# First feed forward: the cosine's whole turns by an integer conversion, with h read from PSUM

## The chip, the cores and the metric

The kernel runs on one core of one Trainium2 chip. The metric is device time in microseconds (us) of one execution. Five engines work side by side, each through a queue of its own in order: TensorE (PE; its weight loads are PEld), VectorE (DVE), ScalarE (ACT), GpSimd (POOL) and SyncE (SP), which issues most transfers.

## The reference, cut to what matters

Attention over 4 batches, 8 heads, 576 positions gives x of 2304 tokens by 512. Two feed forwards follow. The change is in the first alone.

```python
def _moe_ref(x, w_in, w_out):          # x (2304, 512), w_in (512, 2048), w_out (2048, 512)
    h = x @ w_in
    g = h * np.cos(h)
    return g @ w_out

def _moe2_ref(x, w_in, w_out, a, b):   # the second feed forward: a rational function of h
    ...
```

[...]

## The kernel before

**Numbers.** Matmuls run in fp32r on operands that are split in a high and a low part, so each product is three matmuls: high by high, high by low, low by high. Weights arrive as 64-bit words; `dec_abs` (L142, ACT) and `dec_ops` (L154, L156, L158, DVE) turn a tile of them into fp32, and `w_split` (L173 on ACT for the high part, L176 on POOL for the low part) splits it.

**Steps.** The first feed forward has 128 steps, g = 0 to 127. A step takes one block of tokens (256, 352 or 288 columns) and one of 16 slices of 128 hidden units. Its parts are, in the letters of the strings that order them:

- `l1` (L419): 12 matmuls give h in a PSUM bank of the tag `h`, which has two banks.
- U or u: u = h/2pi + 0.25, on ACT (L508) or on DVE (L510).
- K or k: hs, a copy of h in SBUF, on ACT (L512) or on DVE (L514). 114 of the 128 steps have it; in the other 14, M reads h itself.
- J or j: t = u + 12582912, which rounds u to a whole number, on ACT (L516, 5 times) or on DVE (L518, 123 times).
- V: u = (t - 12582912) - u on DVE (L520), both operands in SBUF.
- N: the sine on ACT (L522). M: t = sine times hs (or h) on DVE (L524).
- G: gh, the high part of t, on ACT (L528). H or h: gl, the low part, on POOL or on DVE (L530).
- `l2` (L438): 12 matmuls of gh and gl with the second weight, two or three steps later, into the banks y.

Other letters of the string place the decoding and splitting of the first weights (x, y, z, p, q, s, w, a, b) and the attention of the next tokens (T, L). Steps 0 to 31 work on the first two blocks of 256 tokens; the first weights are decoded beside steps 0 to 15, and the attention and the second weights' decoding go on beside later steps. From step 32 on most strings run N, M, G and H of the step before beside U, K, J and V of this one. The order is written out by hand in `ORD`, `C_ORD`, `AB_ORD` and `REST`; a letter acts on the first pending step that has not had it and whose forerunner by `NEED` is done. Buffers rotate in pools: u, t and hs have two buffers each, and an instruction that writes a buffer or a bank waits for the last one that used it. The program never lets DVE and ACT into one PSUM bank at once, reads included.

From step 128 the second feed forward runs (L466 to L492); the change does not touch its steps.

Of the kernel before, what the change touches and what calls it, by code (L numbers as in the profile page):

```python
# [8 lines left out]
F32 = mybir.dt.float32  # L9
F32R = mybir.dt.float32r  # L10
I32 = mybir.dt.int32
BF16 = mybir.dt.bfloat16
AF = mybir.ActivationFunctionType
ALU = mybir.AluOpType
AX = mybir.AxisListType

B, H, S, D = 4, 8, 576, 64
# [3 lines left out]
NF = DFF // 128  # L21
# [12 lines left out]
NB2 = 384  # L34
# [17 lines left out]
LV1 = (3, 4)  # L52
PL1 = []
AB_ORD = "UKjVTswxyzNMabpqGHL"
NEED = {"J": "U", "V": "J", "N": "V", "M": "N", "G": "M", "H": "G"}
REST = "swNMUKjVGhTL"
C_ORD = {}
ORD = {}
for _g in (0, 1, 23):
    ORD[_g] = "ukjVTswxyzNMabpqGHL"  # L60
NPRE = 4
EVB, STB = 4, 6
LATE_OE = False
# [3 lines left out]
NCONST = C_ID + 128  # L67
TWO_PI = 6.2831850
INV_2PI = 1.0 / (2.0 * math.pi)
MAGIC = 12582912.0  # L70
LN_SHIFT = 2.0 ** -63


# [17 lines left out]
def attention_moe_moe_kernel(ctx: ExitStack, tc: tile.TileContext, qk0, qk, vv, w1, w2, consts, a, b, out):  # L91
    nc = tc.nc
    ACT, DVE, POOL, PE, SP = nc.scalar, nc.vector, nc.gpsimd, nc.tensor, nc.sync
# [4 lines left out]
    ep = ctx.enter_context(tc.tile_pool(name="ep", bufs=2))  # L98
# [13 lines left out]
    biases = const.tile([128, 4], F32, name="biases")  # L112
# [300 lines left out]
    def l1(bk, f):  # L413
        d = blocks[bk]
        n, cs = d["n"], slice(d["xcol"], d["xcol"] + d["n"])
        h = bank("a" if d["ph"] == 2 and f % 2 else "h")
        ops = [(w, x, c) for c in range(KD) for w, x in ((wh, xh), (wh, xl))] + [(wl, xh, c) for c in range(KD)]
        for k, (w, x, c) in enumerate(ops):
            PE.matmul(h[:, :n], w[d["ph"], f, 0][:, 128 * c:128 * c + 128], x[c][:, cs], start=k == 0, stop=k == len(ops) - 1)  # L419
        return h[:, :n]  # L420
# [19 lines left out]
    def evac(bk):  # L440
        d = blocks[bk]
        n, t0 = d["n"], 0 if bk == bB else d["tok"]
        for c, y in enumerate(d["y"]):
            t = stage("ev")
            if d["ph"] == 2 or bk == bB:
                n = 512
            src = y[:, :n]
            if bk == len(blocks) - 1 and c == len(d["y"]) - 1:
                ACT.activation(out=t[:, :256], in_=src[:, :256], func=AF.Copy)
                DVE.tensor_copy(out=t[:, 256:], in_=src[:, 256:])  # L450
            elif c % 2:
                DVE.tensor_copy(out=t[:, :n], in_=src)  # L452
            else:
                ACT.activation(out=t[:, :n], in_=src, func=AF.Copy)
            if d["ph"] == 1:
                SP.dma_start(out=x2d[:, c, t0:t0 + n], in_=t[:, :n])
            else:
                (ACT if bk == len(blocks) - 1 and c == len(d["y"]) - 1 else SP).dma_start(out=out[t0 + 128 * c:t0 + 128 * c + 128, :], in_=t)
# [37 lines left out]
    def ew_new(g, bk, h):  # L496
        n = blocks[bk]["n"]
        e = dict(g=g, h=h)
        for k in ("u", "t", "hs"):
            e[k] = ep.tile([128, NB2], F32, tag=k, name=k)[:, :n]  # L500
        for k in ("gh", "gl"):
            e[k] = None
        return e

    def ew_op(c, e):
        u, t, hs, h = e["u"], e["t"], e["hs"], e["h"]
        if c == "U":
            ACT.activation(out=u, in_=h, func=AF.Identity, scale=INV_2PI, bias=biases[:, 2:3])  # L508
        elif c == "u":
            DVE.tensor_scalar(out=u, in0=h, scalar1=INV_2PI, scalar2=0.25, op0=ALU.mult, op1=ALU.add)  # L510
        elif c == "K":
            ACT.activation(out=hs, in_=h, func=AF.Copy)  # L512
        elif c == "k":
            DVE.tensor_copy(out=hs, in_=h)  # L514
        elif c == "J":
            ACT.activation(out=t, in_=u, func=AF.Identity, bias=biases[:, 3:4])  # L516
        elif c == "j":
            DVE.tensor_scalar(out=t, in0=u, scalar1=MAGIC, scalar2=None, op0=ALU.add)  # L518
        elif c == "V":
            DVE.scalar_tensor_tensor(out=u, in0=t, scalar=MAGIC, in1=u, op0=ALU.subtract, op1=ALU.subtract)  # L520
        elif c == "N":
            ACT.activation(out=u, in_=u, func=AF.Sin, scale=-TWO_PI)  # L522
        elif c == "M":
            DVE.tensor_tensor(out=t, in0=u, in1=hs if "K" in e else h, op=ALU.mult)  # L524
        elif c == "G":
            n = t.shape[1]
            e["gh"], e["gl"] = (gp.tile([128, NB2], F32R, tag=k, name=k)[:, :n] for k in ("gh", "gl"))
            ACT.activation(out=e["gh"], in_=t, func=AF.Copy)  # L528
        else:
            (POOL if c == "H" else DVE).tensor_tensor(out=e["gl"], in0=t, in1=e["gh"].bitcast(F32), op=ALU.subtract)  # L530
            state["g", e["g"]] = e["gh"], e["gl"]

# [118 lines left out]
    def order(g):  # L651
        return ORD[g] if g in ORD else AB_ORD if g < 2 * NF else C_ORD[g % (2 * NF)] if g % (2 * NF) in C_ORD else REST
# [9 lines left out]
    def run_steps(p, g0, g1):  # L662
        for g in range(g0, g1):
            bk = None
            if g < len(steps):
                bk, f = steps[g]
                h = l1(bk, f)
            if state["evac"]:
                evac(state["evac"].pop())
            run("early", g)  # L670
            if g < N1:
                todo = decs.pop(g, ())
                e = ew_new(g, bk, h)
                fifo = {c: state["e"] + [e] if c in "NMGH" else [e] for c in "UKJVNMGH"}
                state["e"].append(e)
                for c in order(g):
                    if c.upper() in fifo:
                        for x in fifo[c.upper()]:
                            if c.upper() not in x and NEED.get(c.upper(), "U") in x | {"U": 1}:
                                x[c.upper()] = True  # L680
                                ew_op(c, x)
                                break
                    elif c in "sS":
                        split1(0, POOL if c == "s" else DVE)
                    elif c in "wW":
                        split1(1, POOL if c == "w" else DVE)
                    elif c in "xyzpq":
                        if c == "x":
                            for _, tm in todo:
                                dec_ops(0, *tm)  # L690
                        else:
                            i = "yzpq".index(c)
                            if i % 2 < len(todo):
                                dec_ops(1 + i // 2, *todo[i % 2][1])
                    elif c in "ab":
                        for k in dplan.get(g + 1, ())["ab".index(c):][:1]:
                            w_abs(g + 1, k)
                    elif c == "T":
                        run("pe1", g)
                        run("pe1e", g)  # L700
                    elif c == "L":
                        run("late", g)
                state["e"] = [x for x in state["e"] if "H" not in x]
                state["dec"] = todo
            else:
                for x in state["e"]:
                    for c in "NMGH":
                        if c not in x:
                            ew_op(c, x)
                state["e"] = []  # L710
                second(g, LAG)
                if g == N1:
                    nc.scalar.preload_act_table_set("natural_log_exp_and_others")
                prev = state.pop("prev", None)
                if prev is not None:
                    ew_b(*prev)
                if state["evac"]:
                    evac(state["evac"].pop())
                if bk is not None:
                    state["prev"] = ew_a(p, bk, h)  # L720
                if prev is not None:
                    gh = ew_c(*prev[:2])
                if bk is not None:
                    ew_r(*state["prev"])
                if prev is not None:
                    state["g", g - 1] = ew_d(*prev[:2], gh)
                run("pe1", g)
                run("pe1e", g)
                run("late", g)
            if g < N1:  # L730
                second(g, LAG_AB if bk <= bB else LAG)
            run("pe2", g)
            run("load", g)

    state = {"evac": [], "l2": 0, "e": []}
    dplan = {}
    for k in range(NPRE, NF):
        dplan[DSTEP[k - NPRE]] = pairs[k]
    with tc.manual_schedule():
        with tc.tile_pool(name="att", bufs=2) as p:  # L740
# [1 line left out]
            DVE.memset(msk16, 0.0)  # L742
            DVE.memset(biases[:, 1:2], -63.0 * math.log(2.0))
            DVE.memset(biases[:, 2:3], 0.25)
            DVE.memset(biases[:, 3:4], MAGIC)
            wb = bank("a")
            ms = {}

# [181 lines left out]
```

## Time and profile before

| | |
|---|---|
| median of 3 runs | 993.06 us (992.69 to 993.42) |
| the profiled execution | 990.51 us |
| its span, first to last instruction | 988.7 us |
| busy: PE, DVE, ACT, POOL | 925.2, 786.6, 670.8, 287.5 us |

The span leaves 1.8 us of the profiled execution outside. Busy time is the time in which an engine has an instruction of the program under way; a DVE instruction that is held up inside counts as busy. In the timeline a row is start, duration, engine, line, operation, tiles and shape; in square brackets stands how long the engine had been idle and what it waited for.

### The profile page before, as it was taken

The numbers are of one execution on the slowest core, as the hardware profiler recorded it, in microseconds if no ns is written. First come the engines' busy times: TensorE is split into PE (matmuls) and PEld (weight loads), VectorE is DVE, ScalarE is ACT, GpSimd is POOL, SyncE is SP. The second block draws the span as 40 slices with busy tenths as digits, with TensorE's granted clock in tenths as the row PEclk, the third lists the DMA queues.
The fourth block names the chain that finished last, engine by engine and source line by source line (L and its number), as shares of the span: only waits on it lengthen the run. The fifth ranks groups of instructions, "written<-read, shape, count | busy, mean of one in ns | idle before, by whom it ended". The sixth has DMA issues, their size and how long they took to land.

```text
span 988.7 us, 17482 instructions
## 1 busy us (share of the span) xinstructions
PE 925.2 (94%) x6367; PEld 861.8 (87%) x6367; DVE 786.6 (80%) x1497; ACT 670.8 (68%) x1444; POOL 287.5 (29%) x279
## 2 busy tenths in 40 slices
PE   7557889999999989999899999999999999999997
PEld 6557789998999989999899988888888898898896
DVE  5999986688677787777878898877787778777776
ACT  5765557565475565765757887777777777777775
POOL 2466552213212122121222223223223232232221
PEclk9778999999999999999999999999999999999999
DMA  9745200443423534234325620010010100100000
GB/s 312 254 168 216 62 22 9 148 159 109 138 86 128 172 138 160 89 128 151 128 60 178 188 78 1 2 64 1 6 60 1 51 14 1 65 1 0 33 1 32
DMA packets 51526, 89.36 MB, mean 90 GB/s; under 512 B 4584, under 2 KB 28400, under 8 KB 51440
## 3 DMA queue, kind: packets, MB, share of 16 engines
q1 hardware_dynamic: 50720, 86.58, 26.6%
q10 hardware_dynamic: 720, 1.67, 0.5%
q8 instruction: 50, 0.82, 0.3%
q14 instruction: 36, 0.29, 0.1%
HBM read 70.40 MB, written 17.83 MB: 89 GB/s over the span
## 4 chain that ended last, share of the span: by engine, by line
DVE 32%; PE 26%; ACT 22%; POOL 10%; issue 7%; DMA 3%; POOLq 0%; SPq 0%; ACTq 0%; DVEq 0%
PE h L419 11%; PE y L438 10%; POOL z L478 9%; DVE r L481 7%; ACT r L477 6%; ACT r L476 5%; ACT gh L487 4%; DVE h L482 3%; DVE dec L156 3%; DVE a L482 3%; DVE t L524 3%; DVE dec L158 2%; PE a L259 2%; DVE u L520 2%; DVE t L518 2%
## 5 line engine op out<-in xcount | busy, mean ns | idle before, releaser
L419 PE MATMUL h<-xh,w 128*128 128x288 f32 (+3 forms) x1408 | 339.5, 313 | 9.2 <-DVE hs L514 4.4
L419 PEld LDWEIGHTS h<-xh,w 128*128 128x128 f32 x1408 | 246.2, 191 | 14.6 <-DVE hs L514 4.6
L438 PE MATMUL y<-gh,w 128*128 128x288 f32 (+2 forms) x1024 | 231.3, 302 | 4.5 <-ACT gh L528 4.5
L419 PE MATMUL h<-xl,w 128*128 128x288 f32 (+3 forms) x704 | 207.9, 311 | 0.0
L438 PE MATMUL y<-w,gh 128*128 128x512 f32 x576 | 196.1, 393 | 5.6 <-DVE ev L452 4.3
L478 POOL TENSOR_TENSOR z<-q,r 128x384 f32<-128x384 f32 x96 | 97.3, 1013 | 297.3 <-ACT r L477 293.9
L438 PEld LDWEIGHTS y<-gh,w 128*128 128x128 f32 x1024 | 173.6, 191 | 5.2 <-ACT gh L528 5.2
L438 PE MATMUL y<-gl,w 128*128 128x288 f32 (+2 forms) x512 | 153.6, 300 | 6.0 <-POOL gl L530 5.6
L419 PEld LDWEIGHTS h<-xl,w 128*128 128x128 f32 x704 | 135.6, 193 | 1.8
L438 PEld LDWEIGHTS y<-w,gh 128*128 128x128 f32 x576 | 108.2, 188 | 27.9 <-DVE ev L452 6.8
L481 DVE SCALAR_TENSOR_TENSOR r<-z,r 128x384 f32<-128x384 f32 x96 | 69.5, 724 | 73.3 <-POOL z L478 73.3
L530 POOL TENSOR_TENSOR gl<-t,gh 128x288 fp32r<-128x288 f32 (+2 forms) x67 | 64.1, 957 | 197.4 <-ACT gh L528 180.9
L438 PE MATMUL y<-w,gl 128*128 128x512 f32 x288 | 114.8, 399 | 5.0 <-DVE gl L492 4.8
L419 PE MATMUL a<-xh,w 128*128 128x384 f32 x384 | 106.3, 337 | 0.0
L508 ACT ACTIVATE u<-h,biases 128x288 f32<-128x288 f32 (+2 forms) x116 | 57.2, 494 | 72.2 <-PE h L419 69.2
L438 PEld LDWEIGHTS y<-gl,w 128*128 128x128 f32 x512 | 97.8, 191 | 9.1 <-POOL gl L530 8.4
L528 ACT ACTIVATE gh<-t 128x288 fp32r<-128x288 f32 (+2 forms) x128 | 56.8, 443 | 54.6 <-DVE t L524 54.0
L518 DVE TENSOR_SCALAR t<-u 128x288 f32<-128x288 f32 (+2 forms) x123 | 53.2, 432 | 45.8 <-ACT u L508 44.3
L522 ACT ACTIVATE u<-u 128x288 f32<-128x288 f32 (+2 forms) x128 | 56.7, 443 | 43.7 <-DVE u L520 43.5
L524 DVE TENSOR_TENSOR t<-u,hs 128x288 f32<-128x288 f32 (+2 forms) x114 | 62.9, 552 | 23.8 <-ACT u L522 23.4
L520 DVE SCALAR_TENSOR_TENSOR u<-t,u 128x288 f32<-128x288 f32 (+2 forms) x128 | 74.2, 580 | 6.2 <-ACT t L516 2.0
L419 PEld LDWEIGHTS a<-xh,w 128*128 128x128 f32 x384 | 70.5, 188 | 1.8
(115 smaller groups left out, 1645.3 us busy)
## 6 DMA issues: line engine op xcount, KB each, us to landing
raw<-in_w_dram SPq DMA_DIRECT2D x63, 512.0 KB
qk<-in_qk_dram SPq DMA_DIRECT2D x18, 481.0 KB
wf<-dec SPq DMA_DIRECT2D x32, 256.0 KB
wf<-wf SPq DMA_DIRECT2D x32, 256.0 KB
x2s<-x2d SPq DMA_DIRECT2D x24, 192.0 KB
out_dram<-ev SPq DMA_DIRECT2D x17, 256.0 KB
v<-in_vv_dram SPq DMA_DIRECT2D x16, 240.0 KB
v<-in_vv_dram SPq DMA_DIRECT2D x24, 157.5 KB
```

What stands on the lines that cost most here:

```text
L419: PE.matmul(h[:, :n], w[d["ph"], f, 0][:, 128 * c:128 * c + 128], x[c][:, cs], start=k == 0, stop=k == len(ops) - 1)
L438: PE.matmul(y, l, r, start=first and i == 0 and bk != bB, stop=last and i == 2 and bk != bA)
L477: ACT.activation(out=r, in_=r, func=AF.Exp, scale=-1.0, bias=biases[:, 1:2])
L478: POOL.tensor_tensor(out=z, in0=q, in1=r, op=ALU.mult)
L481: DVE.scalar_tensor_tensor(out=r, in0=z, scalar=2.0, in1=r, op0=ALU.subtract, op1=ALU.mult, reverse0=True)
L482: DVE.scalar_tensor_tensor(out=h, in0=h, scalar=ab[:, 0:1], in1=r, op0=ALU.add, op1=ALU.mult)
L508: ACT.activation(out=u, in_=h, func=AF.Identity, scale=INV_2PI, bias=biases[:, 2:3])
L518: DVE.tensor_scalar(out=t, in0=u, scalar1=MAGIC, scalar2=None, op0=ALU.add)
L520: DVE.scalar_tensor_tensor(out=u, in0=t, scalar=MAGIC, in1=u, op0=ALU.subtract, op1=ALU.subtract)
L524: DVE.tensor_tensor(out=t, in0=u, in1=hs if "K" in e else h, op=ALU.mult)
L528: ACT.activation(out=e["gh"], in_=t, func=AF.Copy)
L530: (POOL if c == "H" else DVE).tensor_tensor(out=e["gl"], in0=t, in1=e["gh"].bitcast(F32), op=ALU.subtract)
```

## The change

J is dropped: U (or u) now writes its result as a 32-bit integer, into the buffer of t, and V takes that integer from h/2pi, reading h from PSUM for the second time. The sine gets scale 2pi and a bias of a quarter turn from a column of `biases`. In steps 0 to 31 the letters K and k are taken out of the order string, so that M reads h from PSUM there; from step 32 on they stay. The letters J and j stay in the strings and do nothing. hs is allocated only where it is written.

```diff
--- before.py
+++ after.py
@@ -52,12 +52,13 @@
 LV1 = (3, 4)
 PL1 = []
 AB_ORD = "UKjVTswxyzNMabpqGHL"
-NEED = {"J": "U", "V": "J", "N": "V", "M": "N", "G": "M", "H": "G"}
+NEED = {"J": "U", "V": "U", "N": "V", "M": "N", "G": "M", "H": "G"}
 REST = "swNMUKjVGhTL"
 C_ORD = {}
 ORD = {}
 for _g in (0, 1, 23):
     ORD[_g] = "ukjVTswxyzNMabpqGHL"
+COPY = {ord(c): None for c in "Kk"}
 NPRE = 4
 EVB, STB = 4, 6
 LATE_OE = False
@@ -67,7 +68,6 @@
 NCONST = C_ID + 128
 TWO_PI = 6.2831850
 INV_2PI = 1.0 / (2.0 * math.pi)
-MAGIC = 12582912.0
 LN_SHIFT = 2.0 ** -63
 
 
@@ -496,37 +496,35 @@
     def ew_new(g, bk, h):
         n = blocks[bk]["n"]
         e = dict(g=g, h=h)
-        for k in ("u", "t", "hs"):
+        for k in ("u", "t"):
             e[k] = ep.tile([128, NB2], F32, tag=k, name=k)[:, :n]
-        for k in ("gh", "gl"):
-            e[k] = None
         return e
 
+
     def ew_op(c, e):
-        u, t, hs, h = e["u"], e["t"], e["hs"], e["h"]
+        u, t, h = e["u"], e["t"], e["h"]
+        k = t.bitcast(I32)
         if c == "U":
-            ACT.activation(out=u, in_=h, func=AF.Identity, scale=INV_2PI, bias=biases[:, 2:3])
+            ACT.activation(out=k, in_=h, func=AF.Identity, scale=INV_2PI, bias=biases[:, 2:3])
         elif c == "u":
-            DVE.tensor_scalar(out=u, in0=h, scalar1=INV_2PI, scalar2=0.25, op0=ALU.mult, op1=ALU.add)
-        elif c == "K":
-            ACT.activation(out=hs, in_=h, func=AF.Copy)
-        elif c == "k":
-            DVE.tensor_copy(out=hs, in_=h)
-        elif c == "J":
-            ACT.activation(out=t, in_=u, func=AF.Identity, bias=biases[:, 3:4])
-        elif c == "j":
-            DVE.tensor_scalar(out=t, in0=u, scalar1=MAGIC, scalar2=None, op0=ALU.add)
+            DVE.tensor_scalar(out=k, in0=h, scalar1=INV_2PI, scalar2=0.25, op0=ALU.mult, op1=ALU.add)
+        elif c in "Kk":
+            e["hs"] = ep.tile([128, NB2], F32, tag="hs", name="hs")[:, :t.shape[1]]
+            if c == "K":
+                ACT.activation(out=e["hs"], in_=h, func=AF.Copy)
+            else:
+                DVE.tensor_copy(out=e["hs"], in_=h)
         elif c == "V":
-            DVE.scalar_tensor_tensor(out=u, in0=t, scalar=MAGIC, in1=u, op0=ALU.subtract, op1=ALU.subtract)
+            DVE.scalar_tensor_tensor(out=u, in0=h, scalar=INV_2PI, in1=k, op0=ALU.mult, op1=ALU.subtract)
         elif c == "N":
-            ACT.activation(out=u, in_=u, func=AF.Sin, scale=-TWO_PI)
+            ACT.activation(out=u, in_=u, func=AF.Sin, scale=TWO_PI, bias=biases[:, 3:4])
         elif c == "M":
-            DVE.tensor_tensor(out=t, in0=u, in1=hs if "K" in e else h, op=ALU.mult)
+            DVE.tensor_tensor(out=t, in0=u, in1=e.get("hs", h), op=ALU.mult)
         elif c == "G":
             n = t.shape[1]
             e["gh"], e["gl"] = (gp.tile([128, NB2], F32R, tag=k, name=k)[:, :n] for k in ("gh", "gl"))
             ACT.activation(out=e["gh"], in_=t, func=AF.Copy)
-        else:
+        elif c in "Hh":
             (POOL if c == "H" else DVE).tensor_tensor(out=e["gl"], in0=t, in1=e["gh"].bitcast(F32), op=ALU.subtract)
             state["g", e["g"]] = e["gh"], e["gl"]
 
@@ -673,7 +671,7 @@
                 e = ew_new(g, bk, h)
                 fifo = {c: state["e"] + [e] if c in "NMGH" else [e] for c in "UKJVNMGH"}
                 state["e"].append(e)
-                for c in order(g):
+                for c in order(g).translate(COPY if g < 2 * NF else {}):
                     if c.upper() in fifo:
                         for x in fifo[c.upper()]:
                             if c.upper() not in x and NEED.get(c.upper(), "U") in x | {"U": 1}:
@@ -742,7 +740,7 @@
             DVE.memset(msk16, 0.0)
             DVE.memset(biases[:, 1:2], -63.0 * math.log(2.0))
             DVE.memset(biases[:, 2:3], 0.25)
-            DVE.memset(biases[:, 3:4], MAGIC)
+            DVE.memset(biases[:, 3:4], 0.25 * TWO_PI)
             wb = bank("a")
             ms = {}
```

## Rows read from the trace of the kernel before

**Rows 1.** Busy us by stretch: PE, PEld, DVE, ACT, POOL; clock, DMA share, GB/s.

```profile
...
43.00:134.00 91.00, 66.84 (x502) 61.36 (x503) 87.91 (x136) 49.73 (x112) 55.20 (x44) 0.87 0.38 128
...
216.00:575.00 359.00, 349.39 (x2865) 342.65 (x2866) 280.70 (x581) 232.61 (x526) 80.11 (x82) 1.00 0.40 130
...
```

**Rows 2.** The chain that ended last, 43 to 134 us: start, duration, what.

```profile
...
43.83 0.33 DVE hs L514
...
132.90 1.10 PE y L438 x7
```

**Rows 3.** J, V and M by line: nanoseconds minimum/median/maximum, first and last start, forms.

```profile
...
L518 DVE TENSOR_SCALAR t<-u x123: 277/310/1378, 44.1 to 561.8; 128x288 f32<-128x288 f32 x78, 128x256 f32<-128x256 f32 x29, 128x352 f32<-128x352 f32 x16
...
L520 DVE SCALAR_TENSOR_TENSOR u<-t,u x128: 424/459/1550, 44.4 to 562.1; 128x288 f32<-128x288 f32 x80, 128x256 f32<-128x256 f32 x32, 128x352 f32<-128x352 f32 x16
...
L524 DVE TENSOR_TENSOR t<-u,hs x114: 383/450/1456, 47.2 to 564.4; 128x288 f32<-128x288 f32 x76, 128x256 f32<-128x256 f32 x23, 128x352 f32<-128x352 f32 x15
L524 DVE TENSOR_TENSOR t<-u,h x14: 407/422/509, 53.9 to 457.6; 128x256 f32<-128x256 f32 x9, 128x288 f32<-128x288 f32 x4, 128x352 f32<-128x352 f32 x1
...
```

**Rows 4.** DVE busy time in 43 to 134 us: line 518, then line 520.

```profile
...
43.00:134.00 91.00, 9.35 (x16) 0.87 0.38 128
...
43.00:134.00 91.00, 14.99 (x17) 0.87 0.38 128
...
```

**Rows 5.** Timeline of step 6: DVE, then POOL, then PE.

```profile
...
87.08 1.38 DVE L518 TENSOR_SCALAR t<-u 128x256 f32<-128x256 f32 x1
88.50 1.39 DVE L520 SCALAR_TENSOR_TENSOR u<-t,u 128x256 f32<-128x256 f32 x1
...
91.01 0.41 DVE L524 TENSOR_TENSOR t<-u,hs 128x256 f32<-128x256 f32 x1
...
86.83 2.77 POOL L176 TENSOR_TENSOR w<-dec,w 128x512 fp32r<-128x512 f32 x2 [0.34 <-ACT w L173]
...
87.96 0.28 PE L419 MATMUL h<-xh,w 128*128 128x256 f32 x1
...
91.93 0.39 PE L438 MATMUL y<-gh,w 128*128 128x256 f32 x1 [2.38 <-ACT gh L528]
...
```

**Rows 6.** ACT by line and form: busy us, mean ns of one, idle before.

```profile
...
L522 ACT ACTIVATE u<-u 128x256 f32<-128x256 f32 x32 | 13.2, 416 | 23.3 <-DVE u L520 23.2
...
L516 ACT ACTIVATE t<-u,biases 128x256 f32<-128x256 f32 x3 | 1.5, 504 | 0.0
...
```

**Rows 7.** Who waited for whom in 43 to 134 us: us, times, longest.

```profile
...
DVE t L524 <- ACT u L522: 1.9, 4, 0.5
...
```

**Rows 8.** M of step 0, l1 of 2; M of 31, l1 of 33.

```profile
...
47.22 0.41 DVE L524 TENSOR_TENSOR t<-u,hs 128x256 f32<-128x256 f32 x1
...
44.21 0.58 PE L419 MATMUL h<-xh,w 128*128 128x256 f32 x1 [4.35 <-DVE hs L514]
...
188.98 0.42 DVE L524 TENSOR_TENSOR t<-u,hs 128x256 f32<-128x256 f32 x1
...
188.27 0.41 PE L419 MATMUL h<-xh,w 128*128 128x352 f32 x1
...
```

**Rows 9.** Timeline rows of steps 37, 38 and 40, 57 and 55.

```profile
...
211.11 0.46 ACT L512 ACTIVATE hs<-h 128x352 f32<-128x352 f32 x1 [1.03 <-DVE u L510]
...
219.52 0.53 DVE L520 SCALAR_TENSOR_TENSOR u<-t,u 128x352 f32<-128x352 f32 x1
...
218.12 0.32 PE L419 MATMUL h<-xh,w 128*128 128x352 f32 x1
...
292.23 0.40 PE L419 MATMUL h<-xh,w 128*128 128x288 f32 x1 [0.86 <-ACT hs L512]
...
292.74 0.45 DVE L524 TENSOR_TENSOR t<-u,h 128x288 f32<-128x288 f32 x1
...
```

**Rows 10.** Timeline: U of step 44 on ACT, H of step 42 on POOL.

```profile
...
238.61 0.54 ACT L508 ACTIVATE u<-h,biases 128x352 f32<-128x352 f32 x1
...
240.54 1.24 POOL L530 TENSOR_TENSOR gl<-t,gh 128x352 fp32r<-128x352 f32 x1
...
```

## The prediction

> **What bounds the kernel now.** I read the busy time by stretch first. From 43 to 134 us, steps 0 to 17, DVE is busy for 87.9 of 91 us and PE for 66.8, so PE idles 24.2 us; POOL is busy for 55.2. From 216 to 575 us PE is busy for 349.4 of 359 us [rows 1]. The chain of work that ended last agrees: between its pieces at 43.83 and 132.90 us it runs mostly over DVE, and it goes over to PE at 132.90 [rows 2]. So before 134 us less DVE work is time, if nothing else takes over; after that PE sets the pace and at most the 9.6 us that it idles can be had.
>
> Next the form of DVE's work in that first stretch. J's shortest run is 277 ns and V's 424, but both reach 1.4 to 1.5 us [rows 3]. In the stretch 16 J take 9.35 us and 17 V take 14.99 [rows 4]; at their shortest they would take 4.4 and 7.2, so 12.7 us is being held up. Step 6 shows by what: POOL's two weight splits run from 86.83 to 89.60; J (0.28 of work) lasts 1.38 until the first of them is through, V lasts until 89.89, 0.29 after the second [rows 5]. M with hs from SBUF reaches 1456 ns, M with h from PSUM never more than 509 in 14 runs [rows 3]. I read this as: a DVE instruction that reads both operands, or one at double rate, from SBUF is held while a POOL instruction runs, and one with an operand in PSUM is not.
>
> **J goes.** 16 times in the stretch. What it waited for POOL is not gained: the next DVE instruction in order (a decoding step with both operands in SBUF) meets the same POOL instruction. I count its own 0.28 us: 16 x 0.28 = 4.5 us. Bounds: 0, if each lies in time that DVE would wait anyway, and 9.35, if the waits vanish too [rows 4].
>
> **V reads h from PSUM.** Its length I take unchanged: M costs the same from either memory, medians 422 and 450 ns, and at its shortest 24 ns more from PSUM [rows 3]. An integer operand is one more conversion on the way in; no row has that pair, and I take 0. What changes is that V runs while POOL does. Where it was held, only the 0.29 us after POOL's release comes off the path [rows 5], since the wait again passes on. V's excess of 7.8 us [rows 4] at 0.97 apiece (1.39 less 0.42) is 8 held Vs at least; smaller holds make it about 10: 10 x 0.29 = 2.9 us. Bounds: a loss of 17 x 0.02 = 0.4 and a gain of 7.8. [...] The trace shows 24 ns on M. [...]
>
> **K and k go in steps 0 to 31.** On DVE one copy in the stretch lies on the chain: 0.33 us [rows 2], taken as 0.3. The others are on ACT, which is busy for 49.7 of 91 us [rows 1], so behind DVE they are worth nothing by themselves. That the Ms are no longer held passes on as above; I take 0.
>
> **N gets a bias from SBUF.** The same form with and without one: J on ACT 504 ns, N 416 [rows 6], 88 ns more. It is hidden unless DVE stands waiting for the sine, 4 times in the stretch [rows 7]: -0.4 us. Bounds 0 and 17 x 0.088 = 1.5. U's integer output on ACT has no row; taken as the same.
>
> **h's bank is held longer.** There are two banks, so l1 of step g+2 waits for the last reader of h in step g. Without the copy that is M in steps 0 to 31. In the trace of before, M ends after l1 of g+2 starts in 9 steps, by 14.0 us in all; the first is step 0 (47.63 against 44.21, where PE had already waited for the copy), the last step 31 (189.40 against 188.27) [rows 8]. Mostly this takes the place of a wait that PE has anyway. In step 6 M ends at 91.42, so the 12 matmuls of l1 (1.43 us) would move from 87.96 to 91.4; but PE then stood from 89.55 to 91.93 for G of step 6, and its l2 needs H after that [rows 5]. Matmuls slide into an idle stretch. And M itself comes earlier, by J and by V's hold. I take -0.8 of a possible -14.0 us.
>
> From step 32 on the copy stays, but V reads h last. In order strings with K before V, V now waits for K, since the two engines are kept apart on one bank (K of step 37 stands idle for 1.03 us until u on DVE, which reads the same h, is through [rows 9]); K's 0.3 us takes J's place, so V is no later. Where DVE is late, PE waits: l1 of step 40 starts at 218.12 and V of 38 ends at 220.05; l1 of step 57 starts at 292.23 in the bank that a copy had just freed, while M of 55 ends at 293.19 [rows 9]. Steps 36, 38, 55 and 87 together: 0.7 + 1.9 + 1.0 + 1.0 = 4.6 us, less what V gains. Against it stand the 9.6 us of PE idle from 216 to 575 us [rows 1], which come of DVE being late in just those places; there J (0.3) and V's hold go too. I call it even: 0, between -4.6 and +5.
>
> **U writes t's buffer.** U of step g must now wait for H of g-2, which reads t; before, J did, on DVE. What queues behind U on ACT is K, G and the attention's copies. Only in step 44 is this long: U at 238.61, H of 42 on POOL ends at 241.78, 3.2 us [rows 10]. POOL's H there stands behind DVE work that comes earlier by two Js and Vs; taken as 0, at worst -3.2.
>
> **Sum.** 4.5 + 2.9 + 0.3 - 0.4 - 0.8 = 6.5 us off the profiled execution: 990.5 - 6.5 = 984.0 us (its span 988.7 becomes 982.2). The median of the runs is 2.55 us above the profiled one, so the forecast is 993.06 - 6.5 = 986.6, given as 986.5 us.
>
> **Rivals.**
>
> *More.* The waits for POOL vanish instead of passing on: J's 9.35 and V's 7.8, less 1.5 for N: 15.7 us, 977.4 us. For it: PE idles 24.2 us in the stretch, so there is room. Against: in step 6 each POOL instruction holds one DVE instruction, and the decoding that comes next would be held as well. Chance 0.15; it counts from 982 us down.
>
> *Nothing.* POOL's instructions in turn with the decoding set the pace, busy for 55.2 us against DVE's decoding; the freed time becomes idle time in front of the decoding. Then only what DVE does when POOL is idle counts: half of J's 4.5 and the copy, less 0.8 and 0.4: 1.4 us, 991.7 us. Chance 0.11.
>
> *Slower.* PE waits for h's banks: 14.0 us in steps 0 to 31 and 4.6 us later, uncovered, against 7.7 - 0.4 = 7.3 gained: 11.3 us, 1004 us. It decides once more than 9.3 of the 18.6 us fall where PE was not waiting. For it: from step 18 on PE hardly waits at all, and there is no idle stretch to slide into. Against: of the 14.0 us over 10 lie in steps 0, 6 and 15, where PE was waiting, and Ms come earlier. Chance 0.12.
>
> **Numbers.** Forecast 0.62. A measurement of this kernel can tell about 0.2%, 2 us, from no change. Faster than 991.1: the forecast, More, and a part of Nothing, 0.80. Within: 0.08. Slower than 995.0: the third rival, 0.12. The range 978 to 992 us leaves out the third rival and the far end of More. The forecast's own range is 982 to 991.
>
> **What would show it.** In the profile after: no instruction of line J; V under 0.6 us at its longest where it was 1.55; DVE busy in 43 to 134 us shorter by some 10 us; the hand-over of the chain from DVE to PE near 127 instead of 133 us; N at 504 ns for 256 columns; new waits of PE for V or M in front of l1, under 1 us in all before 134 us and near steps 33, 40, 57 and 89; PE's idle time after 216 us about as before. The prediction is wrong if the decoding's lines grow by what J and V lose, if V takes 0.5 us or more, or if PE's waits for l1 sum to more than 5 us.

## The result and the profile after

| | before | after |
|---|---|---|
| median | 993.24 us (992.69 to 994.88, 4 runs) | 978.58 us (978.38 to 978.66, 4 runs) |
| the profiled execution | 990.51 us | 978.61 us |
| its span | 988.7 us | 976.8 us |

The ratio is 0.9849, with a 95% interval of 0.9832 to 0.9866: 14.7 us faster, where 6.5 were forecast. The direction and the range (978 to 992) held; the size was more than twice the forecast. Run again beside other kernels, the changed kernel took 979.93 us against 993.86, a ratio of 0.9861 (0.9845 to 0.9877); one of the seven runs of before beside it was a slow one, 1282.80 us, which the ratio leaves out. The two profiled executions differ by 11.9 us.

Busy time by stretch, columns as in [rows 1]:

```profile
43.00:134.00 91.00, 72.39 (x581) 68.92 (x582) 82.07 (x135) 53.45 (x115) 61.46 (x50) 0.89 0.38 127
...
216.00:575.00 359.00, 350.21 (x2859) 342.24 (x2858) 248.10 (x498) 240.99 (x529) 84.79 (x81) 1.00 0.40 131
```

In the first stretch DVE is busy 5.8 us less and PE 5.6 us more: more steps fit into it. After 216 us DVE has lost 32.6 us and PE's idle time went only from 9.6 to 8.8 us.

The chain that ended last (start, duration, what), where it goes over to PE:

```profile
121.45 0.34 DVE t L522
121.79 0.04 issue
121.83 1.68 PE h L419 x12
```

The hand-over is at 121.83, 11.1 us earlier than before [rows 2] and some 5 us before the forecast's 127. In the kernel before, the chain's rows from 121.87 to the hand-over stand under POOL. But POOL's gap there is a wait for ACT's gh, and gh had waited 2.22 us for DVE's M, so DVE's lateness set that end too:

```profile
130.65 0.41 DVE L524 TENSOR_TENSOR t<-u,hs 128x256 f32<-128x256 f32 x1
...
131.59 1.26 POOL L530 TENSOR_TENSOR gl<-t,gh 128x256 fp32r<-128x256 f32 x1 [2.02 <-ACT gh L528]
```

From l1 of step 8 to l1 of step 16 alone the time fell from 36.97 to 29.80 us, more than half of the gain. V and M by line, columns as in [rows 3] (there is no row of J's):

```profile
L518 DVE SCALAR_TENSOR_TENSOR u<-h,t x128: 407/457/527, 43.8 to 550.1; 128x288 f32<-128x288 f32 x80, 128x256 f32<-128x256 f32 x32, 128x352 f32<-128x352 f32 x16
...
L522 DVE TENSOR_TENSOR t<-u,hs x91: 431/456/1454, 183.0 to 552.5; 128x288 f32<-128x288 f32 x76, 128x352 f32<-128x352 f32 x15
...
L522 DVE TENSOR_TENSOR t<-u,h x37: 382/420/510, 46.8 to 446.8; 128x256 f32<-128x256 f32 x32, 128x288 f32<-128x288 f32 x4, 128x352 f32<-128x352 f32 x1
```

No V is longer than 527 ns, where 1550 occurred [rows 3]; M is held only where it still reads hs. V's sum in 43 to 134 us is now:

```profile
43.00:134.00 91.00, 8.28 (x20) 0.89 0.38 127
```

That is 0.41 us each, where 17 took 14.99 us [rows 4]. The timeline of step 6, DVE and then POOL, shows it beside [rows 5]:

```profile
82.77 0.42 DVE L518 SCALAR_TENSOR_TENSOR u<-h,t 128x256 f32<-128x256 f32 x1
83.11 3.11 DVE L156 SCALAR_TENSOR_TENSOR dec<-raw,dec 128x512 int32<-128x512 int32 x2
86.14 0.41 DVE L522 TENSOR_TENSOR t<-u,h 128x256 f32<-128x256 f32 x1
...
82.31 3.36 POOL L176 TENSOR_TENSOR w<-dec,w 128x512 fp32r<-128x512 f32 x2
```

POOL's two splits run from 82.31 to 85.67. V starts 0.46 us into them and runs its 0.42 us beside them. Then two decoding steps, whose shortest is 0.65 us, take 3.11 us: the hold did pass on to them, as the forecast had it, but V and the time it would have stood are through by then. The three decoding lines in 43 to 134 us, count | busy, mean ns, before:

```profile
L156 DVE SCALAR_TENSOR_TENSOR dec<-raw,dec 128x512 int32<-128x512 int32 x24 | 21.4, 926 | 0.0
L158 DVE SCALAR_TENSOR_TENSOR dec<-raw,dec 128x512 int32<-128x512 int32 x24 | 18.5, 811 | 0.0
L154 DVE TENSOR_SCALAR dec<-dec 128x512 int32<-128x512 int32 x24 | 15.9, 692 | 0.4
```

and after:

```profile
L156 DVE SCALAR_TENSOR_TENSOR dec<-raw,dec 128x512 int32<-128x512 int32 x24 | 24.3, 1044 | 0.0
L158 DVE SCALAR_TENSOR_TENSOR dec<-raw,dec 128x512 int32<-128x512 int32 x24 | 19.5, 850 | 0.0
L154 DVE TENSOR_SCALAR dec<-dec 128x512 int32<-128x512 int32 x24 | 18.1, 794 | 0.1
```

They grew by 6.1 us (61.9 against 55.8) while J's 9.35 us went and V's time fell by 6.7 with three more Vs in the stretch. J and V had been held for 12.7 us there. So a part of the held time passed on, and a part is gone. Over steps 0 to 31 it is the same: J, V and M were held for 18.4 us before and for 1.3 after, and the decoding's lines for 17.7 and then 23.7, so some 6 of 17 us went over to them. How much of the rest is time gained, the experiments tell.

### The profile page after: what moved, and what is told of

Same layout as the page of the kernel before. It is cut to its first block, busy times and chain, and to the rows that moved or that the text cites. A ratio compares the mean times of both kernels' runs of the same rounds, so it can differ in the third digit from the quotient of the medians.

```text
span 976.8 us, 17279 instructions
## 1 busy us (share of the span) xinstructions
PE 921.2 (94%) x6367; PEld 860.5 (88%) x6367; DVE 727.9 (75%) x1369; ACT 674.8 (69%) x1421; POOL 292.4 (30%) x279
## 4 chain that ended last, share of the span: by engine, by line
PE 36%; DVE 25%; ACT 21%; POOL 10%; issue 6%; DMA 2%; POOLq 0%; ACTq 0%; DVEq 0%
PE h L419 16%; PE y L438 15%; POOL z L478 9%; DVE r L481 7%; ACT r L477 6%; ACT r L476 5%; ACT gh L487 5%; DVE h L482 3%; DVE dec L156 3%; DVE a L482 3%; PE a L259 2%; PE a L374 2%; DVE dec L158 2%; DVE t L522 1%; PE a L355 1%
## 5 line engine op out<-in xcount | busy, mean ns | idle before, releaser
L419 PE MATMUL h<-xh,w 128*128 128x288 f32 (+3 forms) x1408 | 338.6, 312 | 18.5 <-DVE t L522 16.3
L528 POOL TENSOR_TENSOR gl<-t,gh 128x288 fp32r<-128x288 f32 (+2 forms) x67 | 67.4, 1006 | 191.6 <-ACT gh L526 165.4
L508 ACT ACTIVATE t<-h,biases 128x288 int32<-128x288 f32 (+2 forms) x116 | 57.6, 497 | 87.8 <-PE h L419 77.0
L518 DVE SCALAR_TENSOR_TENSOR u<-h,t 128x288 f32<-128x288 f32 (+2 forms) x128 | 58.1, 454 | 75.8 <-ACT hs L514 60.8
L520 ACT ACTIVATE u<-u,biases 128x288 f32<-128x288 f32 (+2 forms) x128 | 67.8, 530 | 21.0 <-DVE u L518 20.7
L438 PEld LDWEIGHTS y<-w,gl 128*128 128x128 f32 x288 | 54.0, 188 | 19.6 <-DVE gl L492 11.7
L522 DVE TENSOR_TENSOR t<-u,hs 128x288 f32<-128x288 f32 (+1 forms) x91 | 50.5, 555 | 25.6 <-ACT u L520 24.9
```

The source lines that it names most:

```text
L438: PE.matmul(y, l, r, start=first and i == 0 and bk != bB, stop=last and i == 2 and bk != bA)
L508: ACT.activation(out=k, in_=h, func=AF.Identity, scale=INV_2PI, bias=biases[:, 2:3])
L518: DVE.scalar_tensor_tensor(out=u, in0=h, scalar=INV_2PI, in1=k, op0=ALU.mult, op1=ALU.subtract)
L520: ACT.activation(out=u, in_=u, func=AF.Sin, scale=TWO_PI, bias=biases[:, 3:4])
L522: DVE.tensor_tensor(out=t, in0=u, in1=e.get("hs", h), op=ALU.mult)
```

## The experiments

Each kernel ran beside the kernel before on one chip; kdead, vdead, better2 and again on another chip than the rest. The expectations weigh four theories: A, the gain is made where DVE sets the pace, because J is gone and V is no longer held by POOL; B, it is one DVE instruction less that counts, wherever V reads; C, the copies are what matters; D, much of it is made after step 32. Beside the medians I read from each trace when l1 of step 0 and l1 of step 32 start, since steps 0 to 31 are those that the weights' decoding shares with POOL, and l1 of step 127. Such rows are, in the kernel before and then after:

```profile
35.24 0.39 PE L419 MATMUL h<-xh,w 128*128 128x256 f32 x1
...
185.31 0.33 PE L419 MATMUL h<-xh,w 128*128 128x352 f32 x1
```

```profile
35.77 0.58 PE L419 MATMUL h<-xh,w 128*128 128x256 f32 x1
...
174.28 0.33 PE L419 MATMUL h<-xh,w 128*128 128x352 f32 x1
```

From step 0 to step 32 these took 150.08 us (185.31 less 35.24, rounded) and 138.51.

| kernel | median us | ratio to before (95%) | l1 of 0 to l1 of 32 | 32 to 127 |
|---|---|---|---|---|
| before | 993.2 | | 150.08 | 373.75 |
| after | 978.6 | 0.9849 (0.9832 to 0.9866) | 138.51 | 373.20 |
| again | 979.9 | 0.9861 (0.9845 to 0.9877) | 139.88 | 372.83 |
| first | 982.8 | 0.9898 (0.9883 to 0.9914) | 139.81 | 374.79 |
| rest | 991.7 | 0.9986 (0.9976 to 0.9995) | 149.81 | 373.51 |
| onlyk | 991.8 | 0.9985 (0.9976 to 0.9995) | 149.38 | 375.05 |
| keepk | 983.4 | 0.9909 (0.9892 to 0.9925) | 141.72 | 373.29 |
| kdead | 981.6 | 0.9875 (0.9859 to 0.9891) | 140.23 | 373.66 |
| jfree | 983.5 | 0.9911 (0.9883 to 0.9938) | 142.01 | 373.35 |
| jlock | 988.1 | 0.9950 (0.9934 to 0.9966) | 145.78 | 372.65 |
| vsbuf | 983.9 | 0.9902 (0.9881 to 0.9923) | 143.20 | 373.38 |
| vdead | 981.6 | 0.9884 (0.9866 to 0.9901) | 140.29 | 375.77 |
| kall | 983.5 | 0.9903 (0.9891 to 0.9916) | 142.32 | 372.97 |
| vall | 986.1 | 0.9932 (0.9920 to 0.9943) | 146.03 | 372.91 |
| v2free | 985.0 | 0.9918 (0.9905 to 0.9930) | 145.36 | 372.68 |
| v2lock | 990.1 | 0.9973 (0.9963 to 0.9982) | 149.96 | 372.88 |
| better | 978.9 | 0.9856 (0.9840 to 0.9872) | 139.96 | 370.66 |
| better2 | 980.0 | 0.9866 (0.9848 to 0.9884) | 139.78 | 371.73 |

after, again, first and better2 are the same code in steps 0 to 31 and took 138.5 to 139.9 us there (mean 139.5): a difference under some 1.4 us between two traces says nothing. Most of that spread lies in steps 16 to 23, which take 27.97 us in after, at a granted clock of TensorE of 1.00, and 29.2 to 29.3 in the other three, at 0.94 (the clock is a mean over the stretch: in the trace of after it is 0.50 in 44 to 50 us and 1.00 in 101.5 to 976). Below, "held" is the sum of what an instruction takes over the shortest of its form, over steps 0 to 31; by this count V and M from PSUM come to 0.3 and 1.0 us, though none of them takes over 0.43 us.

### Which steps: first and rest

```diff
+        new = g < 2 * NF        # first;  g >= 2 * NF in rest
-            ACT.activation(out=k, in_=h, func=AF.Identity, ...)
+            ACT.activation(out=k if new else u, in_=h, func=AF.Identity, ...)
...
+        elif c == "j":
+            if not new:
+                DVE.tensor_scalar(out=t, in0=u, scalar1=MAGIC, scalar2=None, op0=ALU.add)
+        elif c == "V" and not new:
+            DVE.scalar_tensor_tensor(out=u, in0=t, scalar=MAGIC, in1=u, op0=ALU.subtract, op1=ALU.subtract)
...
```

Where `new` is false, the sine is the old one too, and in rest the copies stay in steps 0 to 31.

> The whole change, but only in steps 0 to 31; from step 32 on U, J and V stand as before. Theory A (the gain is made in the stretch that DVE bounds, 43 to 134 us, where J is gone and V is no longer held by POOL): 979 to 981 us, 12 to 14 us under before, since the changed kernel's l1 of step 32 already came 11.0 of the 11.9 us earlier. Theory D (much of the gain is made after step 32, where PE sets the pace and the two traces hide it): 985 us or more.

> The reverse: the new U and V only from step 32 on, steps 0 to 31 as before with J and the copies. Theory A: within 2 us of before. Theory D: 5 us or more under before. If V behind K costs more than J's going gives back there: up to 4.6 us over before.

first took 982.8 us, 10.4 under before: between the two theories' numbers, nearer to A. rest took 991.7, 1.5 under it, within A's 2 us. Together that is 11.9 us. In steps 0 to 31 first gained all there is to gain (139.81 us) and rest nothing. After step 32 there is a small gain as well, but the last column shows it only roughly: first and onlyk, which have the old letters there, lost time while the granted clock was low (steps 72 to 75 took 17.65 us at 0.90 and 18.03 at 0.91), and so did vdead, the one kernel with the new letters that took over 373.7 (375.77; its steps 56 to 59 took 17.69 us at 0.90, the clock falling after PE had waited 1.89 us in front of l1 of step 57; in kdead, with the same wait, 16.19 at 1.00). Steps 72 to 75 at a clock of 1.00, before and then after:

```profile
350.67:367.71 17.04, 14.37 (x123) 13.84 (x121) 14.30 (x29) 11.11 (x26) 4.39 (x5) 1.00 0.30 107
```

```profile
340.35:356.24 15.89, 14.43 (x124) 13.87 (x122) 12.09 (x26) 11.04 (x24) 4.89 (x5) 1.00 0.32 114
```

All kernels with the new U and V there take 15.9 us in these steps, vsbuf 16.3.

### The copies: onlyk, keepk and kdead

```diff
-                for c in order(g).translate(COPY if g < 2 * NF else {}):
+                for c in order(g):                       # keepk, kdead: the copies stay
...
-            DVE.tensor_tensor(out=t, in0=u, in1=e.get("hs", h), op=ALU.mult)
+            DVE.tensor_tensor(out=t, in0=u, in1=h if e["g"] < 2 * NF else e.get("hs", h), op=ALU.mult)   # kdead
```

onlyk has the old U, J and V, and no copies in steps 0 to 31.

> The one part alone: U, J and V as before everywhere, but no copy of h in steps 0 to 31, so M reads h from PSUM there. Theory A: 989 to 994 us: Ms lose their hold (1.8 us in the stretch, half of it gained), and PE's waits in front of l1 grow by a few us in steps where it waits anyway. Theory C: 985 us or less.

> The new U and V everywhere, but the copies of h stay in steps 0 to 31 where they stood. Theory A: 977 to 981 us; the copies are worth 0.3 us on DVE and cost nothing on ACT, and PE's waits for h's banks (6.75, 2.81 and 2.42 us in front of l1 of steps 2, 8 and 17) become shorter, against Ms that are held again (1.8 us in the stretch). Theory C (the copies were what mattered): 988 us or more.

> The new U and V, and the copies of h made in steps 0 to 31 where they stood, but read by nobody there: M reads h from PSUM as in the changed kernel. Beside the kernel in which M reads the copy (983.4 us) it tells what of the copies costs 4.8 us. M's hold (a hold by POOL that V no longer has is taken by M, whose 11 runs from SBUF are 4.0 us over their shortest in 43 to 134 us there): 978 to 980 us, as the changed kernel. The copies' own time and waits on ACT and DVE: 982 to 984 us.

onlyk 991.8 us: the copies alone are worth 1.4 us, as A said. keepk 983.4 us, above A's 981: with the new V the copies cost some 4 us against the changed kernel. kdead, in which the copies are made but M doesn't read them, is at 981.6 us, between the two numbers expected, and at 140.23, near the 139.5 us. Its ratio lies just clear of keepk's, so where M reads counts. M by line in keepk and then in kdead:

```profile
L522 DVE TENSOR_TENSOR t<-u,hs x114: 384/450/1492, 47.3 to 555.7; 128x288 f32<-128x288 f32 x76, 128x256 f32<-128x256 f32 x23, 128x352 f32<-128x352 f32 x15
```

```profile
L522 DVE TENSOR_TENSOR t<-u,h x37: 379/420/510, 47.8 to 449.9; 128x256 f32<-128x256 f32 x32, 128x288 f32<-128x288 f32 x4, 128x352 f32<-128x352 f32 x1
```

In keepk the 23 Ms from SBUF in steps 0 to 31 are held for 5.0 us in all, where before they were held for 2.9: a part of the hold that V no longer has passes on to M. Reading h there brings 1.5 us (141.72 less 140.23), at the edge of the spread. What of the rest the copies themselves cost, 0.3 to 1.7 us, the spread hides.

### J: jfree and jlock

```diff
+        elif c in "Jj":
+            if e["g"] < 2 * NF:
+                DVE.tensor_scalar(out=u[:, :128], in0=h[:, :128], scalar1=1.0, ...)                 # jfree
+                DVE.tensor_scalar(out=u, in0=cst[:, :u.shape[1]], scalar1=1.0, ...)                 # jlock
```

> The changed kernel with an additional DVE instruction of J's form at J's place in steps 0 to 31 (one f32 operand from SBUF, a constant, 128x256, into u, which V overwrites next; it adds work and the result doesn't depend on it). Theory A: it is held by POOL as J was, up to 1.4 us, and costs 6 to 9 us in all: 985 to 988 us. Theory B: it costs what its 0.28 us costs wherever it reads, as much as the same length from PSUM.

> The changed kernel with an additional DVE instruction at the same place of about J's length that reads 128 columns of h in PSUM into u (it adds work and the result doesn't depend on it). Theory A: it is never held, 0.25 to 0.35 us each, and costs 17 x 0.3 = 5 us at most: 980 to 984 us. Theory B: as the one from SBUF, within 1 us.

The added instruction by line, in jfree and then in jlock:

```profile
L513 DVE TENSOR_SCALAR u<-h x32: 273/281/292, 44.5 to 176.8; 128x128 f32<-128x128 f32 x32
```

```profile
L513 DVE TENSOR_SCALAR u<-cst x32: 276/318/1346, 44.9 to 181.4; 128x256 f32<-128x256 f32 x32
```

At their shortest they are alike, 273 and 276 ns. From PSUM none of 32 is held; from SBUF they are held for 7.0 us. jfree costs 4.2 us by the medians (983.5 against 979.3, the mean of the two of the changed kernel) and 2.5 in steps 0 to 31; jlock 8.8 and 6.3. B is out: the hold is paid in part, 3.8 us of 7.0 in the trace and 4.6 by the medians. Where the other part goes can be seen: the decoding that follows is held for less. Its line 154 over steps 0 to 31, in jfree and then in jlock:

```profile
L154 DVE TENSOR_SCALAR dec<-dec 128x512 int32<-128x512 int32 x28 | 20.6, 771 | 0.2
```

```profile
L154 DVE TENSOR_SCALAR dec<-dec 128x512 int32<-128x512 int32 x28 | 17.1, 650 | 0.1
```

The clock has a share in the 3.8 us. Steps 16 to 23, in jfree and then in jlock, columns as in [rows 1]:

```profile
119.84:148.13 28.29, 25.57 (x215) 25.17 (x213) 20.36 (x48) 14.38 (x31) 13.78 (x14) 1.00 0.05 18
```

```profile
122.32:152.62 30.30, 26.82 (x214) 26.62 (x213) 21.70 (x48) 14.47 (x30) 13.84 (x14) 0.94 0.05 17
```

For the same matmuls PE is busy 1.2 us longer at 0.94 than at 1.00; without that, some 2.5 of the 7.0 us are paid (an estimate). Whether the hold brought the lower clock about, these runs don't tell. The two added instructions differ in one thing more: jfree's must wait for U on ACT and jlock's need not, so some of jlock's time can lie where DVE waits anyway, and the pair would rather show the hold too small.

### V: vsbuf and vdead, then kall and vall, v2free and v2lock

In vsbuf V reads the copy where there is one; vdead is kdead with that V in steps 0 to 31.

```diff
-            DVE.scalar_tensor_tensor(out=u, in0=h, scalar=INV_2PI, in1=k, ...)
+            DVE.scalar_tensor_tensor(out=u, in0=e.get("hs", h), scalar=INV_2PI, in1=k, ...)
```

> The new U and V with all copies kept, and V reads the copy hs from SBUF wherever the step has one (9 or 10 of the 17 steps in 43 to 134 us, nearly all from step 32 on): in those V has two SBUF operands again, as before the change, but J stays away. Theory A: V reaches 1.4 us again, 2 to 5 us over the kernel with the copies and V from PSUM. Theory B (what counts is one DVE instruction less in the chain from U to the sine; where V reads is indifferent): within 1 us of it.

> As the last, but V reads the copy from SBUF in those steps of 0 to 31 that have one, and M reads h from PSUM: so V alone has two SBUF operands again (8 times in 43 to 134 us). V's hold vanishes when it is taken away (as J's): 2 to 4 us over the last kernel. It passes on to the next instruction: within 1 us of it.

By vdead's own marks V's hold passes on. But vsbuf took 1.5 us more than keepk in steps 0 to 31 and 0.5 by the medians; vdead 0.1 more than kdead and nothing by the medians. With V held for 3.3 and 2.8 us in them, half of it is about the spread, so these two leave it open. So the effect was made larger: kall and vall have a copy in each step of 0 to 31, and v2free and v2lock put an instruction of V's form at J's place.

```diff
+        return s if "K" in s or "k" in s else s.replace("U", "UK").replace("u", "uK")              # kall, vall
...
+                DVE.scalar_tensor_tensor(out=u, in0=h, scalar=1.0, in1=cst[:, :u.shape[1]], ...)   # v2free
+                DVE.scalar_tensor_tensor(out=u, in0=cst[:, :u.shape[1]], scalar=1.0, in1=cst[:, :u.shape[1]], ...)   # v2lock
```

> The new U and V; in every step of 0 to 31 ACT or DVE makes a copy of h that nobody reads (behind U where the step had none); M reads h. The base for the next kernel: 980 to 985 us, the copies' time on ACT alone.

> As the last, but V reads the copy from SBUF in all steps of 0 to 31: V has two SBUF operands in all 18 to 20 of its runs in 43 to 134 us, not in 8. If V's hold is paid as J's was (3.8 of 6.4 us held, from l1 of step 0 to l1 of step 32): 3 to 5 us more than the last kernel over those steps. If it passes on to the next instruction: within 1 us.

> The changed kernel with an additional DVE instruction of V's form at J's place in steps 0 to 31, both operands in SBUF (constants; it writes u, which V overwrites next, so it adds work only). If its hold is paid: 987 to 991 us, 3 us or more over the next kernel. If it passes on: as the next, 983 to 986 us.

> The same, with one of the two operands h in PSUM: never held, 0.41 us each. By the one of 0.28 us from PSUM, which cost 2.6 us from l1 of step 0 to l1 of step 32 and 4.5 by the medians: 3.8 us there, 983 to 986 us.

V from the copy in vall (in 20 of the 32 steps, since in the other 12 the copy comes after V):

```profile
L518 DVE SCALAR_TENSOR_TENSOR u<-hs,t x20: 404/734/1476, 45.2 to 181.5; 128x256 f32<-128x256 f32 x20
```

The added instruction in v2free and then in v2lock:

```profile
L513 DVE SCALAR_TENSOR_TENSOR u<-h,cst x32: 407/414/426, 44.3 to 179.8; 128x256 f32<-128x256 f32 x32
```

```profile
L513 DVE SCALAR_TENSOR_TENSOR u<-cst x32: 408/482/1495, 45.0 to 185.1; 128x256 f32<-128x256 f32 x32
```

V in vall is held for 6.7 us; vall took 3.7 us more than kall in steps 0 to 31 and 2.6 by the medians, and the intervals don't overlap. v2lock is held for 8.1 us; it took 4.6 us more than v2free, 5.1 by the medians. (v2free itself cost 5.9 us in those steps, where 3.8 were expected.) So V's hold is paid as J's is: of the time held 54% (3.8 of 7.0, jlock), 55% (3.7 of 6.7, vall) and 57% (4.6 of 8.1, v2lock) comes out at the end of the stretch. That the three agree so well is luck: a pair is good to some 1.4 us; by the medians the shares are 65, 39 and 63%; and in each pair the kernel with the hold has a lower clock in steps 16 to 23 (0.94 against 1.00, then twice 0.89 against 0.94), where PE is busy some 1.2 us longer, and without which the shares would be 36 to 41%. About half is what can be said. Of the rest a good part is seen to pass on: the decoding's lines are held for 3.8 us less in jlock than in jfree, 1.9 less in vall than in kall and 4.1 less in v2lock than in v2free.

### PE's new waits: better and better2, and the changed kernel again

```diff
-                for c in order(g).translate(COPY if g < 2 * NF else {}):
+                for c in order(g).translate(COPY if g < 2 * NF and g not in (0, 6, 15) else {}):   # better
...
-23: 'swNMUjVGhTL'
+23: 'swNMUKjVGhTL'     # both
-38: 'skwNMLUGTjVh'
+38: 'skwNMUGjVLTh'     # better2
```

> The changed kernel, but steps 0, 6 and 15 keep a copy of h on ACT, placed after V, and step 55, 87 and 119's like get one where they had none; so PE need not wait for M in front of l1 of steps 2, 8, 17, 57 and 89, where it waited 6.75, 2.81, 2.42, 1.89 and 1.88 us. Theory A, in which DVE bounds the first stretch: nothing from steps 2, 8 and 17 (PE stands idle later anyway), some of 3.8 us from 57 and 89, where PE sets the pace: 975 to 978 us. If the bank waits cost their whole length: 963 to 968 us.

> The changed kernel with a copy in steps 55, 87 and 119, which had none, and in step 38 V ahead of the attention's softmax (the order of letters is the one edit there). PE waited 1.43, 1.89 and 1.88 us in front of l1 of steps 40, 57 and 89, where it sets the pace. Theory: 2 to 4 us under the changed kernel, 975 to 977 us; if step 38's softmax is then late for PE, no gain there, 977 to 978 us.

> The changed kernel once more, beside the others on one chip: 978 to 979 us if its four runs of before are its level; up to 981 us if they were a good draw, since all kernels that differ from it by one part spread over 2 to 3 us.

In better the copies of steps 0, 6 and 15 stand where they stood in the kernel before, ahead of V (that of step 0 on DVE), not behind it as the expectation says, because the order strings that put them behind V are overwritten further down in the kernel; and step 119 had its copy already. The first matmul of l1 of steps 2, 8, 17, 33, 40 and 57 in the changed kernel, with the wait in front of it:

```profile
47.21 0.58 PE L419 MATMUL h<-xh,w 128*128 128x256 f32 x1 [6.75 <-DVE t L522]
...
86.60 0.39 PE L419 MATMUL h<-xh,w 128*128 128x256 f32 x1 [2.81 <-DVE t L522]
...
121.83 0.39 PE L419 MATMUL h<-xh,w 128*128 128x256 f32 x1 [2.42 <-DVE t L522]
...
178.13 0.43 PE L419 MATMUL h<-xh,w 128*128 128x352 f32 x1 [0.68 <-ACT hs L514]
...
208.45 0.43 PE L419 MATMUL h<-xh,w 128*128 128x352 f32 x1 [1.43 <-DVE u L518]
...
282.31 0.40 PE L419 MATMUL h<-xh,w 128*128 128x288 f32 x1 [1.89 <-DVE t L522]
```

With these copies in better the waits at steps 8 and 17 shrink to 0 and 0.1 us and that at step 2 to 4.0, yet steps 0 to 31 take 139.96 us, no less than without: they are covered. One sees where: from l1 of step 0 to l1 of step 8 better takes 47.79 us against the changed kernel's 50.83, and from there to l1 of step 16 it takes 32.79 against 29.80. What the wait gave back is lost again; how much of that is the copies' own cost, the run doesn't tell. The waits at 57 and 89 go in both kernels, that at 40 in better2, and steps 32 to 127 take 1.1 to 2.5 us less in the traces; by the medians (978.9 and 980.0 us) neither can be told from the changed kernel (978.6 and 979.9), and both miss the 975 to 978 us that were expected. No version beat it.

## Why the prediction was too small

**The step that failed** is the sentence on J, "What it waited for POOL is not gained", and with it V's "since the wait again passes on": they put all but a small part of the held time at nothing. The runs show in its place: of the time that a DVE instruction is held by POOL about half is paid (3.8 of 7.0 us, 3.7 of 6.7 and 4.6 of 8.1), and of the rest a good part passes on to the decoding. V from PSUM runs beside POOL's instruction; only what follows is held, and for less. The rival More, that all of it vanishes, was wrong to the other side. That its 977.4 us lies nearer is luck: it has too large a share of the hold, but only the hold up to 134 us.

- **J**, forecast at 4.5 us: 2.5 for its own time (jfree), and of the 5.3 us that it was held on DVE before half, an estimate of 2.7: 5.2 us. Its own 0.28 us was oversized, the hold missing.
- **V**, forecast at 2.9: in steps 0 to 31 it was held for 10.2 us before, and 15 of 32 Vs by over 0.15 us each. Half of it is an estimate of 5.1 us. In the forecast's stretch 11 of 17 were held, about as many as it counted; what each is worth was too small. That V from PSUM costs no more was right: 407 ns at its shortest against 404 from SBUF in vall and 424 in the old form [rows 3].
- **M**, forecast at 0: held for 2.9 us before; by keepk and kdead (1.5 us paid of 4.0 less held) an estimate of 1.1.
- **N**: its length came as forecast; what it costs the kernel, no run isolates. For 256 columns it takes 504 ns, busy, mean:

```profile
L520 ACT ACTIVATE u<-u,biases 128x256 f32<-128x256 f32 x32 | 16.1, 504 | 13.4 <-DVE u L518 13.4
```

  DVE waits for the sine longer than before [rows 7], since it comes there sooner:

```profile
DVE t L522 <- ACT u L520: 5.3, 7, 0.9
```

- **PE's waits for h's banks**, forecast at 0.8: their places were right (steps 2, 8, 17, 40, 57, 89), and that most is covered (better). "Under 1 us in all before 134 us" was not: the wait at step 2 grew from 4.35 [rows 8] to 6.75, and 2.81 and 2.42 are new. By the forecast's own mark of 5 us that would have made it wrong; but better, which takes most of these waits away and gains nothing there, says that DVE's lateness, not the bank, sets the end there. At step 33 PE waits for step 32's copy, not for M of 31 as the forecast had it. By its own reading the forecast also left out V of steps 39 and 71, which ended 0.7 and 1.0 us after l1 of 41 and 73 started; after the change PE doesn't wait there.
- **U's waits for POOL**, forecast at 0: they are there, 3.3 us in front of the U of 352 columns, and cost nothing that shows: l1 of step 45 starts 10.96 us earlier than before, that of step 40 9.67.

```profile
L508 ACT ACTIVATE t<-h,biases 128x352 int32<-128x352 f32 x13 | 7.2, 554 | 13.8 <-PE h L419 8.6 <-POOL gl L528 3.3 <-DVE hs L516 1.7
```

- **From step 32 on**, forecast as even: 0.6 to 0.9 us gained in the two traces of the changed kernel, 1.5 by the medians of rest. It is made of what the forecast weighed: steps 40 to 43, 72 to 75 and 104 to 111 take 1.0 to 1.2 us less each, steps 32 to 35, 36 to 39, 56 to 59 and 88 to 91 take 0.4 to 0.9 us more each.
- **The sum** of 5.2, 5.1, 1.1 and the copy's 0.3, less 0.4 and 0.8, is 10.5 us for steps 0 to 31, where the traces show 10.6 (150.08 less 139.5). So close an agreement is luck: with a third or with two thirds of the hold paid it would be 8 or 13. With 1 us after step 32 the traces come to 11.6, near the 11.9 us of the two profiled executions. The medians differ by 13.9 to 14.7. One reason is that the profiled execution of before was a short one: l1 of step 0 starts at 35.24 us in it, the earliest of all 18 traces (the others 35.75 to 37.15), and its mean granted clock was 0.984, where most runs of before have 0.974 to 0.981. Time and clock go together there: sixteen runs of before at 0.976 took 993.8 us on average, three at 0.982 took 991.5. The four runs of the changed kernel have 0.984 to 0.990, so some of what the medians gain goes with the clock; why it is higher, no run isolates.

The other marks: no row of J, V under 0.6 us, and PE's idle time after 216 us about as before came as forecast. DVE's busy time in 43 to 134 us fell by 5.8 and not by some 10, because faster steps brought more work into the stretch and the decoding took 6.1 us more; the hand-over of the chain is the better mark.

## What to carry to other kernels

An instruction that is held by another engine can be worth more than its shortest time when it goes or is freed: here its own time and about half of its held time (3.8 of 7.0 us in jlock, 3.7 of 6.7 in vall, 4.6 of 8.1 in v2lock), with a third and two thirds not excluded. "It passes on to the next instruction" needs a look at whether the freed instruction now runs beside the other engine's, which the timeline of before can't show; a pair of added instructions of the same length, one that can be held and one that can't, measures it directly. And the profiled execution of before lay 2.5 us off the median (990.51 against 993.06), so small differences are better read between two points inside the trace, with the granted clock of that stretch beside them.

## What the runs showed of the hardware

V, M and the added instructions were never held by POOL where they had an operand in PSUM (128 Vs up to 527 ns, all wider forms among them; 37 Ms up to 510; 32 of jfree up to 292; 32 of v2free up to 426), and V's form with both operands in SBUF was (up to 1495 ns), as was one with a single fp32 operand in SBUF that runs 256 columns in 276 ns (up to 1346). In the trace of before J, V and M on DVE took over 0.15 us more than the shortest of their form 64 times, each time with a POOL instruction running beside for at least a part of it; in that of after 63 of the 128 Vs had one beside them, and none took over 19 ns more than the shortest of its form. The forecast's "double rate" stands in the trace of before as well: at its shortest J takes 277 ns for 256 columns and 330 for 352, 0.55 ns a column, V 424 and 524, 1.04 ns a column. Of the held time this kernel paid about half (3.8 of 7.0 us, 3.7 of 6.7 and 4.6 of 8.1).

Neither the integer nor the operand in PSUM cost V anything that shows. With the integer it takes 407 ns at its shortest with h from PSUM and 404 with hs (vall); its form with two fp32 operands takes 407 with h from PSUM (v2free) and 408 from SBUF alone (v2lock). The 24 ns that the forecast read as M's cost from PSUM don't show after the change either: at its shortest M takes 382 ns from PSUM there and 379 in kdead, 384 from SBUF in keepk.

The decoding's lines 156 and 158, of one form, take 1044 and 850 ns on average after the change. At their shortest they are alike (652 and 651 ns); 9 of the 24 of line 156 and 6 of the 24 of line 158 took over 0.15 us more than that.
